# A new instruction order for a two-layer attention and FFN kernel, planned with a changed clock for GpSimd's port and for instruction fetches

## The chip, the core and the metric

The kernel runs on one core of a Trainium2 chip. A core has engines that work side by side, each from its own list of instructions: TensorE (PE, matrix products), VectorE (DVE), ScalarE (ACT), GpSimd (POOL), and SyncE (SP), which starts DMA transfers. An engine takes its instructions strictly in the order in which they stand. The metric is the device time of one execution in microseconds (us), the median over several.

## The reference

Two layers, each an attention over 2048 tokens in four segments of 512 tokens, with a memory that is carried from segment to segment, and a gated FFN. 32 heads have 16 values each; the model is 512 wide, the FFN 1792.

```python
for s in range(N):                               # 4 segments of 512 tokens
    qs, ks, vs = (q[:, :, s].copy(), k[:, :, s].copy(), v[:, :, s].copy())
    logits = jnp.einsum('bhqd,bhkd->bhqk', qs, ks) * scale + mask
    p = _softmax(logits, axis=-1)
    a_dot = jnp.einsum('bhqk,bhkd->bhqd', p, vs)
    pq = phi(qs)                                 # where(t > 0, t + 1, exp(t))
    num = jnp.einsum('bhld,bhde->bhle', pq, M)
    den = jnp.einsum('bhld,bhd->bhl', pq, z)[..., None] + 1e-06
    a_mem = num / den
    o = g * a_mem + (1.0 - g) * a_dot
    outs.append(o)
    pk = phi(ks)
    M = M + jnp.einsum('bhld,bhle->bhde', pk, vs)
    z = z + jnp.einsum('bhld->bhd', pk)
...
x = x + _A_ref(_layernorm(x, axis=-1), A_wq, A_wk, A_wv, A_wo, A_beta)
x = x + _B_ref(_layernorm(x, axis=-1), B_w_gate, B_w_up, B_w_down)   # gelu(x @ w_gate) * (x @ w_up) @ w_down
```

Both lines stand twice: the second layer uses the same weights.

## The kernel before

The work of a layer is cut into four segments of 512 tokens, so there are eight attentions (k = 0 to 7) and eight FFNs, numbered alike; k + 4 of the second layer needs the rows that FFN k has finished. All activations stay in the core's memory: `x_sb` holds the running sum, which every output product (`wo`, `down`) is added to.

What an attention k does: a layernorm (`xn`, turned into `xnT` by a DMA or by PE), products for q, k and v, 36 score rounds, taken in pairs, whose exponentials (`pt`) ScalarE makes, masks on `pt` by GpSimd (`affine_select`) or VectorE, and "flushes", products of `pt` with the values. VectorE turns a flush's result (`byq`, `ab`, `aT`). From the second segment of a layer on, the memory's part `amT` is added to `aT`, on VectorE or GpSimd (`on_dve_or_pool`, L1417): these are the sums of attention parts. The memory itself is updated by VectorE in four steps, `macc`, `zacc`, `mblk` and `zcols` (L1286 to L1305). Then come the output products `wo`; their result is added to `x_sb` either by a plain addition with separate statistics (L1463, L856, L859) or, for the first `quick` tiles, by an addition that also sums (L869, `mv` L873) and a square on ScalarE (`junk`, L876). FFN k follows: layernorm, 14 gate products, gelu on ScalarE, 14 up products, 4 output tiles of 14 products.

Nothing of the order is left to a scheduler. The function `order` runs the whole program once against a clock of its own, when the program is built, and emits each instruction when the clock says that its engine would take it. The class `Clocks` holds the time of PE; each other engine is an `Engine` with a list of jobs, from which `serve` takes the one with the least ready time plus slack. Where PE's clock finds no product ready, `order` emits a filling product of 128 columns on the tile `warm`. Three things of this clock matter here.

- A cost that is a `Port` stands for an operation on VectorE or GpSimd that needs the memory port which the planner takes them to share. `serve` lets it start only when the other engine's `port` time has passed (less 0.2 us). A `Port` marked `soft` (second argument) never holds up the other engine; it only makes it 0.15 us longer. A plain number needs no port.
- `Clocks.issue` counts PE's instructions in chunks of 256 (`CHUNK`). At `CHUNK_ASKED` in a chunk the next one is asked for, and at `CHUNK_END` PE waits until what was asked a chunk earlier has had `FETCH` us.
- The slacks and dues are not the same throughout: `POLICY` gives their first values, and `STAGES` a set of others for each window of 20 us (`WINDOW`) of PE's clock; `Policy.move` puts them in force. Among them are `turn_pe` (the FFNs whose `xn` PE turns), `quick`, `at_pool` (what GpSimd's slack is for an addition to `aT`) and `direct` (gates whose gelu reads PSUM).

An order once emitted is fixed. On the chip only semaphores decide when an instruction starts, so an operation that is longer there than in the planner's clock holds up everything behind it on its engine.

Of the kernel before, what the change touches and what calls it, by code (L numbers as in the profile page):

```python
# [37 lines left out]
CHUNK, CHUNK_ASKED, CHUNK_END, FETCH = 256, 178, 222, 3.7  # L38
# [27 lines left out]
def table(halved):  # L66
# [17 lines left out]
    if halved:  # L84
# [31 lines left out]
    rs_pool=32.757, f_urge=-233.244, quick=2, paired=8, turn_pe=1, turn_last=0, w_at=29.345, w_gap=2.17,  # L116
# [8 lines left out]
    park=3)  # L125
# [7 lines left out]
        rs_pool=2.667, quick=6, turn_pe=0, kb_slack=55.298, mem_slack=-32.756, e_q=-2.851, gelu_slack=-0.49,  # L133
        gate_step=78.038, up_due=-98.977, up_step=25.491, down_step=-53.827, upd_due=91.729, vz_slack=14.093,
        x_dve=7.459, direct=6, gelu_tiles=2, look=2.764, lag=0.475, xn_pool=30.206, cut_pool=102.189,
        at_pool=-237.424, gate_due=8.415, starve=1.292, soon=7.146, park=5)),
    (3, 4, dict(
        rs_pool=4.794, turn_pe=12, kb_slack=51.509, mem_slack=58.674, e_q=50.036, e_k=1.445, gelu_slack=1.935,
        gate_step=78.038, up_due=-96.513, up_step=85.14, down_step=-56.495, vz_slack=40.138, x_dve=6.187, direct=6,
        look=2.618, xn_pool=30.206, cut_pool=118.125, at_pool=-208.534, gate_due=14.291, shun=21.0, early=101.394,  # L140
        starve=0.321, soon=7.146, park=2)),
    (4, 5, dict(
        rs_pool=-2.341, quick=0, turn_pe=12, kb_slack=85.554, mem_slack=58.674, qk_due=1.009, e_q=50.137, e_k=1.464,
        gelu_slack=0.429, gate_step=79.294, up_due=-96.513, up_step=84.505, down_step=-72.139, vz_slack=51.333,
        x_dve=6.187, direct=3, gelu_tiles=2, xn_pool=20.238, cut_pool=148.746, at_pool=-208.534, gate_due=8.415,
        shun=21.0, early=101.394, starve=0.453, soon=7.146, park=2)),
    (5, 6, dict(
        rs_pool=36.794, quick=0, turn_pe=12, kb_slack=66.017, mem_slack=58.674, qk_due=1.009, e_q=55.15, e_k=2.984,
        gelu_slack=-0.805, gate_step=79.294, up_due=-96.513, down_step=-70.89, vz_slack=18.865, x_dve=7.455,
        gelu_tiles=2, look=2.835, lag=0.71, xn_pool=20.238, cut_pool=148.746, at_pool=-208.534, gate_due=0.276,  # L150
        shun=21.488, soon=7.146)),
    (6, 7, dict(
        rs_pool=11.417, f_urge=-261.392, quick=0, paired=11, turn_pe=0, flush_wait=0.581, piece_slack=36.524,
        kb_slack=76.591, mem_slack=-10.427, qk_due=-0.609, e_q=97.288, e_k=-5.757, exp_slack=-18.942, e_slack=69.536,
        phi_slack=30.587, gelu_slack=0.965, act_evict=1.166, gate_step=33.55, up_due=-80.509, down_due=-55.61,
        down_step=-81.567, upd_due=143.06, kb_act=60.08, vz_slack=4.039, x_dve=18.331, direct=0, gelu_tiles=2,
        look=2.622, lag=0.754, xn_pool=-3.088, kb_pool=116.679, cut_pool=153.155, at_pool=-189.709, gate_due=0.226,
        shun=85.539, hold=8, early=169.131, starve=0.31, near=101.522, cap=11, soon=0.694, kd_slack=37.99, park=6)),
    (7, 8, dict(
        rs_pool=-52.581, f_urge=-61.761, quick=3, paired=0, turn_pe=13, flush_wait=-3.039, piece_slack=92.516,  # L160
        kb_slack=220.906, mem_slack=57.517, qk_due=-30.647, e_q=-54.782, e_k=89.983, exp_slack=-17.861,
        e_slack=55.594, phi_slack=96.482, gelu_slack=214.751, act_evict=-149.173, gate_step=5.34, up_due=-0.69,
        up_step=3.923, down_due=12.354, down_step=-3.42, upd_due=-3.412, kb_act=75.691, vz_slack=-199.522,
        x_dve=3.843, direct=4, gelu_tiles=6, look=1.342, lag=0.004, xn_pool=-28.912, kb_pool=53.965, cut_pool=27.06,
        at_pool=-56.962, gate_due=-1.429, shun=104.852, hold=14, early=6.432, starve=57.777, near=-2.631, cap=0,
        soon=-55.855, kd_slack=-7.989, park=5)),
    (8, 9, dict(
        rs_pool=-52.581, f_urge=-145.617, quick=3, paired=0, turn_pe=9, flush_wait=-5.724, piece_slack=95.692,
        kb_slack=220.647, mem_slack=59.145, qk_due=-29.873, e_q=-54.782, e_k=89.76, exp_slack=-17.752,
        e_slack=55.641, phi_slack=95.445, gelu_slack=218.63, act_evict=-149.173, gate_step=5.34, up_due=-2.89,  # L170
        up_step=10.443, down_due=12.354, down_step=-3.42, upd_due=-3.412, kb_act=75.691, vz_slack=-188.382,
        x_dve=3.864, direct=5, gelu_tiles=6, lag=0.004, xn_pool=-26.431, kb_pool=53.965, cut_pool=27.06,
        at_pool=-56.962, gate_due=-1.429, shun=104.852, hold=14, early=6.432, starve=57.777, near=-2.631, cap=0,
        soon=-86.977, kd_slack=-7.989, park=5)),
    (9, 10, dict(
        rs_pool=-12.084, f_urge=-80.924, paired=7, turn_pe=0, flush_wait=-10.54, piece_slack=101.497,
# [20 lines left out]
        kd_slack=-0.609, park=5)),  # L197
# [1809 lines left out]
```

## Time and profile before

| | us |
|---|---|
| median of 3 executions | 538.3 (537.09 to 540.27) |
| the profiled execution | 536.81 |
| its span, first to last instruction | 535.1 |
| PE busy in it | 525.1 |
| ScalarE busy | 445.9 |
| VectorE busy | 433.7 |
| GpSimd busy | 268.1 |

The span is what the trace covers; the profiled execution's own time is 1.7 us longer. Matmuls are pipelined: one is shown busy until its modelled end while the next already runs, so busy PE is not PE at its peak, and a short pause can hide in it. In a row of the timeline the columns are start, duration, engine, line, operation, out<-in, and count, with the idle time before it and what ended that. In a row of groups they are line, engine, operation, shapes and count, then busy us and mean ns, then idle time before and its releasers. L541 is the line of a helper through which all products go, so PE's rows are told apart by their tiles. PE's granted clock was 1.00 throughout.

### The profile page before, as it was taken

The page shows a single profiled execution, that of the slowest core. Times are in us where ns is not written, and L with a number is a line of the kernel's source. Part 1 is how long each engine was busy: PE and PEld are TensorE (multiplying, and loading weights), DVE is VectorE, ACT ScalarE, POOL GpSimd, SP SyncE. Part 2 cuts the span into 40 slices and gives each one's busy share as a digit, 9 for nine tenths or more (in the row PEclk, how much of TensorE's full clock was granted, in tenths as well). Part 3 has the DMA queues.
Part 4 walks back from the last instruction along what each step waited for, and adds up shares of the span by engine and source line. Part 5 has one row for each costly group of instructions (what it writes and reads, how often), then busy time and mean ns, then how long its engine had stood idle before and what let it go on. Part 6 is the DMA issues. An engine that isn't in the chain of part 4 may idle for free.

```text
span 535.1 us, 24177 instructions
## 1 busy us (share of the span) xinstructions
PE 525.1 (98%) x10697; PEld 276.3 (52%) x10697; DVE 433.7 (81%) x823; ACT 445.9 (83%) x598; POOL 268.1 (50%) x333
## 2 busy tenths in 40 slices
PE   9999989998999999999999999999999999999997
PEld 4454455444545454555564544555555456555554
DVE  6899996999997999879987788888977997586342
ACT  6999989887999989899898899799989988952320
POOL 2986472568541966528773366491654354500000
PEclk9999999999999999999999999999999999999999
DMA  8366940323231232201221113310260132102101
GB/s 268 76 121 139 215 141 4 69 41 73 44 60 24 49 55 42 33 12 25 51 44 31 25 24 32 61 34 1 52 103 3 33 51 52 24 2 51 33 2 41
DMA packets 76762, 29.99 MB, mean 56 GB/s; under 512 B 61042, under 2 KB 76658, under 8 KB 76658
## 3 DMA queue, kind: packets, MB, share of 16 engines
q1 hardware_dynamic: 76368, 28.20, 26.0%
q8 instruction: 83, 1.36, 1.0%
q10 hardware_dynamic: 290, 0.26, 0.1%
q14 instruction: 21, 0.17, 0.1%
HBM read 9.70 MB, written 2.10 MB: 22 GB/s over the span
## 4 chain that ended last, share of the span: by engine, by line
PE 77%; DVE 4%; ACT 3%; POOL 1%; issue 1%; DMA 0%; ACTq 0%
PE ps L541 77%; ACT pt L1864 1%; ACT gel_sb L1616 1%; POOL kx L726 1%; DVE xn L920 1%; ACT gel_sb L1519 1%; POOL e L1170 1%; ACT gel_sb L779 0%; DMA xnT<-xn 0%; DVE x_sb L1463 0%; DVE st L856 0%; DVE mblk L1286 0%; DVE byq L1391 0%; DVE x_sb L869 0%; ACT L1519 0%
## 5 line engine op out<-in xcount | busy, mean ns | idle before, releaser
L1864 ACT ACTIVATE pt<-ps 128x1024 bf16<-128x1024 f32 x288 | 278.9, 1036 | 26.8 <-PE ps L541 19.9
L1813 POOL TENSOR_SCALAR_AFFINE_SELECT pt<-pt 128x256 bf16<-128x256 bf16 (+1 forms) x192 | 113.6, 604 | 148.0 <-ACT pt L1864 145.6
L541 PE MATMUL ps<-xnT,wg_sb 128*32 128x512 bf16 (+3 forms) x1367 | 107.7, 362 | 0.3 <-DMA xnT<-xn 0.3
L541 PE MATMUL ps<-wd_sb,gel_sb 128*32 128x512 bf16 (+2 forms) x1431 | 106.1, 354 | 0.0
L541 PE MATMUL ps<-xnT,wu_sb 128*32 128x512 bf16 (+1 forms) x1252 | 103.6, 379 | 0.2 <-ACT gel_sb L1519 0.2
L1557 DVE TENSOR_TENSOR gel_sb<-gel_sb,ps 128x512 bf16<-128x512 bf16 x112 | 75.2, 683 | 30.8 <-PE ps L541 28.5
L541 PEld LDWEIGHTS <-gel_sb 128*32 128x32 bf16 (+1 forms) x1623 | 53.2, 97 | 41.2 <-issue 2.2
L541 PEld LDWEIGHTS <-wu_sb 128*32 128x32 bf16 (+1 forms) x1252 | 45.8, 97 | 45.3 <-issue 2.0
L541 PEld LDWEIGHTS <-wg_sb 128*32 128x32 bf16 (+1 forms) x1367 | 47.5, 97 | 38.7 <-issue 1.5
L1391 DVE STREAM_TRANSPOSE byq<-ps 128x512 f32<-128x512 f32 x64 | 45.4, 710 | 24.5 <-PE ps L541 23.8
L1170 POOL TENSOR_SCALAR e<-e 128x512 bf16<-128x512 bf16 x32 | 50.0, 1565 | 7.1 <-ACT e L1147 6.4
L1463 DVE TENSOR_TENSOR x_sb<-x_sb,ps 128x512 bf16<-128x512 bf16 (+1 forms) x54 | 34.0, 635 | 17.8 <-PE ps L541 17.7
L1818 POOL TENSOR_SCALAR_AFFINE_SELECT pt<-pt 64x1024 bf16<-64x1024 bf16 x32 | 38.1, 1192 | 17.8 <-ACT pt L1864 15.6
L541 PE MATMUL ps<-xnT,wk_sb 128*32 128x512 bf16 (+2 forms) x330 | 34.9, 377 | 0.7 <-ACT pt L1864 0.7
L541 PE MATMUL ps<-pt,vaug 128*32 128x256 bf16 (+2 forms) x1344 | 35.1, 239 | 0.1
L541 PE MATMUL ps<-wv_sb,xnT 128*32 128x512 bf16 (+1 forms) x227 | 32.4, 380 | 2.2 <-DVE x_sb L1463 1.8
L541 PE MATMUL ps<-xnT,wq_sb 128*32 128x512 bf16 (+2 forms) x339 | 34.0, 377 | 0.0
L1616 ACT ACTIVATE gel_sb<-gel_sb 128x1024 bf16<-128x1024 bf16 (+4 forms) x31 | 33.3, 1157 | 0.0
L541 PE MATMUL ps<-q,kx 32*128 32x64 bf16 (+2 forms) x1120 | 31.4, 217 | 0.6 <-ACT pt L1864 0.3
L541 PEld LDWEIGHTS <-vaug 128*32 128x32 bf16 x1344 | 27.2, 97 | 9.2 <-issue 1.6
L856 DVE BATCH_NORM_STATS2 st<-x_sb 128x6 f32<-128x512 bf16 x46 | 31.2, 679 | 0.4
L541 PEld LDWEIGHTS <-kx 32*128 32x128 bf16 x1120 | 16.8, 92 | 28.1 <-issue 27.4
(128 smaller groups left out, 722.1 us busy)
## 6 DMA issues: line engine op xcount, KB each, us to landing
vz<-vaug SPq DMA_DIRECT2D x14, 136.0 KB, 3.0
wg_sb<-in_B_w_gate_dram SPq DMA_DIRECT2D x8, 224.0 KB, 4.0
wu_sb<-in_B_w_up_dram SPq DMA_DIRECT2D x8, 224.0 KB, 3.9
wd_sb<-in_B_w_down_dram SPq DMA_DIRECT2D x7, 256.0 KB, 5.7
x_sb<-in_A_x_dram SPq DMA_DIRECT2D x3, 512.0 KB, 6.5
out_dram<-x_sb SPq DMA_DIRECT2D x12, 128.0 KB, 1.9
xnT<-xn SPq DMA_TRANSPOSE x56, 2.5
kx<-kf SPq DMA_DIRECT2D x12, 64.0 KB, 3.3
```

The lines of the kernel that those rows point to most:

```text
L541: self.nc.tensor.matmul(*args, **kw)
L726: return lambda: eng.tensor_scalar(out=kx[:, :, C * which:C * which + n], in0=kf[:, :, 0:n], scalar1=masks[:, which:which + 1], scalar2=No ...
L856: nc.vector.bn_stats(out=self.st6[:, 0, :], in_=x_sb[:, self.tt0 + j, :])
L920: eng.tensor_scalar(out=xn[:], in0=x_sb[:, self.tt0 + j, :], scalar1=self.mv[:, j, 1:2] if self.wide else self.mv[:, j, 0:1], scalar2=self ...
L1170: lambda eng: eng.tensor_scalar(out=e[0][:], in0=e[0][:], scalar1=1.0, scalar2=None, op0=ALU.min), summed)
L1391: nc.vector.transpose(out=(self.byq[:, pars[0], :, :].rearrange("p a c -> p (a c)") if h is None else self.byq[:].rearrange("p u a c -> p ...
L1463: ck.dve.post(ck.made(), slack, (0.15 + 0.00104 * (c1 - c0), lambda: nc.vector.tensor_tensor(out=xt, in0=xt, in1=ps()[:, 0:c1 - c0], op=AL ...
L1557: ck.dve.post(ck.made(), NORMAL, (0.683, lambda: nc.vector.tensor_tensor(out=g, in0=g, in1=ps()[:], op=ALU.mult), lambda t: (ps.read(t), e ...
L1616: return (0.205 + 0.427 * (f1 - f0), lambda: nc.scalar.activation(out=g, in_=g, func=ACT.Gelu_apprx_tanh), lambda t: self.gelu_done(t, f0, ...
L1813: nc.gpsimd.affine_select(out=view, in_=view, pattern=[[0, 4], [0, n], [1, C]], compare_op=ALU.is_ge, fill=0.0, base=C, channel_multiplier=-1)
L1818: nc.gpsimd.affine_select(out=view, in_=view, pattern=[[0, 4 * TPS], [1, C]], compare_op=ALU.is_ge, fill=0.0, base=0, channel_multiplier=-1)
L1864: nc.scalar.activation(out=pt_all[:, s0:s0 + 2, 2 * p:2 * p + 2, :].rearrange("p r h c -> p h r c"), in_=ps_all[:, pair[0]:pair[1] + 1, :] ...
```

## The change

Four entries of the planner's clock are other (`CHUNK_END`, `FETCH` and two costs), and with them the table `STAGES` from its second row on, that is from 40 us of PE's clock. The operations of the program are the same; who does some of them, and the order of nearly all, is not.

```diff
-CHUNK, CHUNK_ASKED, CHUNK_END, FETCH = 256, 178, 222, 3.7
+CHUNK, CHUNK_ASKED, CHUNK_END, FETCH = 256, 178, 216, 4.2
...
     (4, 5, dict(
-        rs_pool=-2.341, quick=0, turn_pe=12, kb_slack=85.554, mem_slack=58.674, qk_due=1.009, e_q=50.137, e_k=1.464,
...
+        rs_pool=26.539, f_urge=-179.403, quick=0, paired=11, turn_pe=14, flush_wait=-38.498, piece_slack=30.144,
...
-                             (0.154, lambda: nc.vector.tensor_tensor(out=zacc[:], in0=zacc[:], in1=self.zk[:],
+                             (Port(0.154), lambda: nc.vector.tensor_tensor(out=zacc[:], in0=zacc[:], in1=self.zk[:],
                                                                      op=ALU.add), kept)]
...
-                    on_dve_or_pool(t, slack, pol.at_pool, Port(0.15 + 0.275 * part), Port(0.16 + 1.0 * part, True), add, there)
+                    on_dve_or_pool(t, slack, pol.at_pool, Port(0.15 + 0.275 * part), Port(0.16 + 1.0 * part), add, there)
```

GpSimd's addition to `aT` thus holds the port in the clock for its whole length, and the sum of `zacc` waits for the port. The new file has eight lines more in the table, so every later line number is eight higher (L1417 is now L1425).

Counted in the two lists: PE has 21,396 rows before and 20,776 now; matmuls on the whole array 1,048 and 1,194, on four column tiles 7,600 and 7,144, on four row tiles 2,049 in both; changes between these 294 and 303; transposes by PE 32 and 48; fillings after the start 13 and 17. GpSimd has 13 and 14 additions to `aT`, VectorE 11 and 10. VectorE copies `kf` from PSUM 17 and 10 times, ScalarE 11 and 18; ScalarE's squares are 14 and 18, its gelus over gathered tiles 31 and 38. SP has 56 and 52 transposing DMAs for `xnT`. Up to PE's matmul 1005 the lists are the same.

The first place is VectorE after attention 1's memory sum. Before, in VectorE's list (`r`, `ab`, `aT`: the flush's result; `xn`: rows of a layernorm):

```order
L1401 RECIPROCAL r<-byq 128x32
L1407 TENSOR_TENSOR ab<-byq,r 128x2x16x16
L1414 STREAM_TRANSPOSE aT<-ab 128x512
L1303 TENSOR_TENSOR macc<-macc,ps 128x128
L920 TENSOR_SCALAR xn<-x_sb,mv,rs 128x512
L1305 TENSOR_TENSOR zacc<-zacc,zk 128x4
L1286 TENSOR_TENSOR mblk<-macc,bd 128x512
L1463 TENSOR_TENSOR x_sb<-x_sb,ps 128x512 x3
```

GpSimd's list at the same place, where the addition waits for the transposed `aT`:

```order
L899 TENSOR_TENSOR rs<-ve,mhalf 128x2
L1813 AFFINE_SELECT pt<-pt 128x4x128
L1417 TENSOR_TENSOR aT<-aT,amT 128x512
L1818 AFFINE_SELECT pt<-pt 64x1024 x2
L1813 AFFINE_SELECT pt<-pt 128x4x64 x2
```

Now the memory's three steps stand ahead of that, in VectorE's list (`phiq`: the q of the memory's product):

```order
L1399 STREAM_TRANSPOSE byq<-ps 128x512
L1471 TENSOR_TENSOR x_sb<-x_sb,ps 128x512
L1311 TENSOR_TENSOR macc<-macc,ps 128x128
L1313 TENSOR_TENSOR zacc<-zacc,zk 128x4
L1294 TENSOR_TENSOR mblk<-macc,bd 128x512
L1159 SCALAR_TENSOR_TENSOR phiq<-q,e 128x512
L1300 TENSOR_TENSOR zcols<-bd,zacc 128x32
```

`macc`, `zacc` and `mblk` follow each other with nothing between, and the `xn` is gone from there. The last flush of attention 1 comes some twenty rows later, in VectorE's list, and two `xn` still stand behind its `aT`, to which GpSimd's addition is tied:

```order
L1409 RECIPROCAL r<-byq 128x32
L1415 TENSOR_TENSOR ab<-byq,r 128x2x16x16
L1422 STREAM_TRANSPOSE aT<-ab 128x512
L928 TENSOR_SCALAR xn<-x_sb,mv,rs 128x512 x2
L1159 SCALAR_TENSOR_TENSOR e,zk<-kf,e 128x512
L877 SCALAR_TENSOR_TENSOR x_sb,rowsum<-ps,x_sb 128x512
L881 TENSOR_TENSOR mv<-rowsum,means 128x2
```

The additions to `x_sb` behind it are now those that also sum.

The second place is PE at the output products of attention 1. Before (`wv_sb`: value products of attention 4; rows between are left out):

```order
L541 MATMUL ps<-wo_sb,aT 128x512
...
L541 MATMUL ps<-q,kx_122 128x192
...
L541 MATMUL ps<-wv_sb,xnT 128x512
...
L541 MATMUL ps<-pt,vz 32x64
...
L541 MATMUL ps<-xnT,wq_sb 32x512
```

Now (`warm`: fillings; `ident`: transposes by PE):

```order
L549 MATMUL ps<-wv_sb,xnT 128x512
...
L549 MATMUL ps<-warm 128x128
...
L549 MATMUL ps<-wo_sb,aT 128x512
...
L549 MATMUL ps<-q,kx_122 128x192
...
L549 MATMUL ps<-warm 32x128
...
L549 MATMUL ps<-xnT,wq_sb 32x512
...
L549 MATMUL ps<-zcols,phiq 32x8
...
L553 MATMUL ps<-ident,xn 128x128
```

Nine fillings stand among the output and value products (in four groups), and FFN 1's four tiles are turned by PE, with 16 transposes, where SP turned them by DMA.

More of the change, by code (lines that the diff above doesn't have):

```diff
@@ L152 @@
-    (6, 7, dict(
[L153 to L158, printed above, removed]
@@ L159 @@
-    (7, 8, dict(
[L160 to L166, printed above, removed]
@@ L167 @@
-    (8, 9, dict(
[L168 to L174, printed above, removed]
```

320 lines of the change are left out of this document (174 added, 146 removed).

## The prediction

> **What bounds the kernel now.** I read the page's busy times first, then the windows, then PE's own waits, then the stretches in which PE waited.
>
> ```profile
> span 535.1 us, 24177 instructions
> PE 525.1 (98%) x10697; PEld 276.3 (52%) x10697; DVE 433.7 (81%) x823; ACT 445.9 (83%) x598; POOL 268.1 (50%) x333
> ...
> 0.00:62.00 62.00, 59.78 (x1004) 30.02 (x1005) 53.06 (x122) 57.15 (x88) 41.00 (x63) 1.00 0.67 158
> 62.00:200.00 138.00, 133.73 (x2693) 68.72 (x2695) 124.87 (x241) 125.47 (x171) 79.03 (x92) 1.00 0.29 62
> 200.00:520.00 320.00, 319.76 (x6738) 170.30 (x6733) 252.35 (x457) 263.29 (x340) 148.06 (x179) 1.00 0.19 35
> 520.00:536.00 16.00, 11.87 (x276) 7.28 (x268) 3.46 (x6) 0.00 (x0) 0.00 (x0) 1.00 0.11 36
> ```
>
> PE is the bound. In the windows the third number is its busy time: 320 us from 200 to 520 hold 0.24 us of idle PE, and 62 to 200 hold 138.00 - 133.73 = 4.27. Up to PE's matmul 1005 (at about 62 us) the two orders are the same, so the 2.22 idle before it stay, and so does the tail after 520, where the last product, its addition and its store end the run. What an order can win is therefore 4.27 + 0.24 = 4.5 us of visible idle, and it must pay for any work that it adds to PE.
>
> ```profile
> PE ps L541 <- DVE x_sb L1463: 1.8, 1, 1.8
> PE ps L541 <- issue: 1.2, 2, 1.0
> PE ps L541 <- ACT pt L1864: 0.5, 2, 0.3
> PE ps L541 <- DMA xnT<-xn: 0.3, 1, 0.3
> ```
>
> These are PE's waits from 62 to 200 (total, times, longest). Two kinds make 3.0 of the 4.27: one wait for VectorE, and two in which PE waited for nothing that the profile shows, which I take for instructions not yet fetched.
>
> **The port.** The wait for VectorE, first VectorE (DVE), then GpSimd (POOL), then PE:
>
> ```profile
> 126.62 1.29 DVE L920 TENSOR_SCALAR xn<-x_sb,mv,rs 128x512 bf16<-128x512 bf16 x1
> 127.83 1.09 DVE L1305 TENSOR_TENSOR zacc<-zacc,zk 128x4 f32<-128x4 f32 x1
> 129.17 1.62 DVE L1286 TENSOR_TENSOR mblk<-macc,bd 128x512 bf16<-128x512 f32 x1
> 130.71 1.27 DVE L1463 TENSOR_TENSOR x_sb<-x_sb,ps 128x512 bf16<-128x512 bf16 x2
> ...
> 126.61 1.15 POOL L1417 TENSOR_TENSOR aT<-aT,amT 128x512 bf16<-128x512 bf16 x1 [0.31 <-DVE aT L1414]
> 127.72 2.53 POOL L1818 TENSOR_SCALAR_AFFINE_SELECT pt<-pt 64x1024 bf16<-64x1024 bf16 x2
> ...
> 127.61 0.40 PE L541 MATMUL ps<-q,kx 32*128 32x64 bf16 x12
> 127.94 1.68 PE L541 MATMUL ps<-wo_sb,aT 128*128 128x512 bf16 x7
> 131.44 1.46 PE L541 MATMUL ps<-wv_sb,xnT 128*128 128x512 bf16 x6 [1.82 <-DVE x_sb L1463]
> ```
> ```profile
> L920 DVE TENSOR_SCALAR xn<-x_sb,mv,rs x58: 330/408/1292, 6.0 to 488.0; 128x512 bf16<-128x512 bf16 x58
> L1305 DVE TENSOR_TENSOR zacc<-zacc,zk x4: 115/156/1087, 127.8 to 408.2; 128x4 f32<-128x4 f32 x4
> L1286 DVE TENSOR_TENSOR mblk<-macc,bd x6: 667/852/1620, 75.9 to 408.9; 128x512 bf16<-128x512 f32 x6
> L1417 POOL TENSOR_TENSOR aT<-aT,amT x13: 1152/1155/1165, 102.0 to 455.1; 128x512 bf16<-128x512 bf16 x13
> ```
>
> Under GpSimd's addition xn took 1.29 against its median 0.408 (+0.88); under the two masks zacc took 1.09 against 0.156 (+0.93) and mblk 1.62 against 0.852 (+0.77). That is 2.58 us on VectorE, whose next work, the additions that empty PSUM banks, then came late by 1.82 for PE. The old planner held the addition for harmless to VectorE and zacc for an operation without the port. The new one knows both, and its order puts macc, zacc and mblk elsewhere. The term is -1.82 at most and 0 at least, for the wait may only move; GpSimd even gets one such addition more, 14 for 13, and behind one of them two xn still follow. I take -1.8, since macc, zacc and mblk now stand one behind the other, ahead of the two flushes there. The Trainium skill (SBUF — State Buffer, section "SBUF: two separate sides") calls the port that the two engines share an exclusive lock for the whole instruction. By that rule xn would have lost all of the addition's remaining 1.14 us, where the row says 0.88; the rule's price per collision is thus the higher one, and the term, a wait of PE that is measured as such, would not change by it.
>
> **Fetches.**
>
> ```profile
> q8 instruction: 83, 1.36, 1.0%
> ...
> 74.92 0.29 PE L541 MATMUL ps<-q,kf 16*128 16x64 bf16 x7
> 76.20 0.36 PE L541 MATMUL ps<-q,kf 16*128 16x192 bf16 x5 [0.99 <-issue]
> ...
> 124.24 0.83 PE L541 MATMUL ps<-wo_sb,aT 128*32 128x512 bf16 x12 [0.21 <-issue]
> ```
>
> 83 packets feed PE's list of 21,396 rows, one for some 258 rows; the list is now 20,776 rows long. A score round was cut in two for 0.99 us, and 0.21 went before a product; both followed many short matmuls. With the rates below, the poorest stretches of 147 matmuls (the planner's distance from asking to needing) held 2.8, 2.9 and 3.3 us of work in the old order after 62 us and 3.4, 4.1 and 4.3 in the new. So the term is -1.2, with 0 as the other bound: a fetch also competes with data.
>
> **What PE gets to do.** Seven products of 512 columns took 1.68 us (row at 127.94), the last of them 0.380:
>
> ```profile
> L541 PE MATMUL ps<-wo_sb,aT 128*128 128x512 bf16 x65 | 15.2, 380 | 0.0
> L545 PE MATMUL ps<-ident,xn 128*128 128x128 bf16 x32 | 3.2, 231 | 0.0
> ```
>
> (1.68 - 0.38) / 6 = 0.217 for 512 columns. Twelve score matmuls, four abreast, are 512 columns; from 127.61 to the next start at 127.94 went 0.33, so a change of the array's tiling cost 0.33 - 0.217 = 0.11. The new order has 16 more transposes by PE (FFN 1's four tiles, which were DMA transposes) and 4 more filling matmuls, 20 x 128 columns = five products: +1.09. It changes tiling 303 times for 294: 9 x 0.11 = +1.0. Products that went from four column tiles to the whole array (456 small matmuls fewer, 114 products) stream the same columns: 0.
>
> **Where PE is let run dry.** Filling matmuls mark places where the planner had nothing for PE. Before, eleven stood in one place, here the last of three groups:
>
> ```profile
> 70.50 0.55 PE L541 MATMUL ps<-warm 128*128 128x128 bf16 x7
> ...
> 71.93 0.29 PE L541 MATMUL ps<-q,kx 32*128 32x64 bf16 x7 [0.26 <-ACT pt L1864]
> ```
>
> Now six are left there and nine stand around attention 4's first values and FFN 1's first products, where the 1.82 were lost. Beside them I put the 0.26 of this row: +0.3, bounds 0 and 1.82 (the old wait, foreseen but not avoided).
>
> **Covered.** VectorE hands seven copies of kf to ScalarE, where four more squares and a finer split of the gelus stand too. By 62 to 200 ScalarE is busy 125.47 of 138.00 and VectorE 124.87; this is hidden as long as the exponentials keep ahead, and the new order spreads them: 384 of the 512 groups of four score matmuls are out after 345 us of PE work, by the rates above, instead of 326. SP's transposes are four fewer. If that cover is gone, PE waits for score banks as it did for 0.5 us in the waits above; I cost it at 0, bounds -0.5 and +1.
>
> **The sum:** +1.09 + 1.0 + 0.3 - 1.8 - 1.2 = -0.6 us on a span of 535.1. The other pauses (4.5 - 3.0 = 1.5) I leave as they are, since each order makes new ones.
>
> **Rivals.**
>
> Faster: all idle after 62 us goes. -4.5 + 2.1 of work = -2.4, and a little more, because part of a pause hides in the modelled end of the product before it: after 127.94 seven products last 7 x 0.217 = 1.52, so PE lost 131.44 - 129.46 = 1.98 where the row says 1.82. Eight pauses of 0.16 make 1.3: -3.7 in all. For it speaks that from 200 to 520 the old planner lost 0.24; against it that in 62 to 200, where VectorE and ScalarE are 90% busy, it could not.
>
> Slower: the chain in front of FFN 1's first products becomes the bound.
>
> ```profile
> L869 DVE SCALAR_TENSOR_TENSOR x_sb<-ps,x_sb 128x512 bf16<-128x512 f32 x14 | 9.6, 683 | 1.2 <-PE ps L541 1.1
> L873 DVE TENSOR_TENSOR mv<-rowsum,means 128x2 f32<-128x2 f32 x14 | 3.0, 214 | 0.5
> L778 DVE CAST vaug<-ps 128x512 bf16<-128x512 f32 x12 | 8.2, 687 | 1.9 <-PE ps L541 1.6 <-ACT pt L1864 0.2
> L1151 DVE SCALAR_TENSOR_TENSOR phiq<-q,e 128x512 bf16<-128x512 bf16 x24 | 18.2, 763 | 0.6 <-POOL e L1170 0.4
> ```
>
> Behind the last output product VectorE's new queue holds one addition (0.683 + 0.214), a copy of values (0.687), a phiq (0.763), a copy of q (about 0.687) and four xn (4 x 0.408): 4.7 us. PE's list holds, from that product to its transposes, four value, eight q and four k products, a flush of 1280 columns and one round of scores: 19.5 x 0.217 and three changes of tiling, 4.6, and sixteen very short denominators. There is hardly any slack, so every xn or phiq that GpSimd's port holds up (about 0.9 each) reaches PE, and ScalarE's square may come late too. Four such collisions, here and at the other segments, give -0.6 + 3.5 = +2.9; from there it is slower. GpSimd's share of 50% speaks for some of them, the planner's better knowledge against four.
>
> No effect of the port's rule: the new waits are as long as the old one, so -1.8 falls away: +1.2, still no change that can be told.
>
> **How the numbers follow.** The profiled execution took 536.81 (its span and 1.7 around it), the three shown 537.09, 538.3 and 540.27; the middle of all four is 537.7, 0.6 under the median shown, and I add to that. The sum gives 537.1, the faster rival 534.0, the slower 540.6, the last 538.9. Chances: sum 0.33, port without effect 0.12, faster 0.25, slower 0.30. A measurement of this kernel tells about 0.5% (2.7 us) from no change, so no change 0.45, faster 0.25, slower 0.30. The likeliest case's own range is 535.6 to 539.5. The range for 8 in 10 is 533 to 542.5: below, all pauses gone and the added work 1 us cheaper; above, five or six collisions.
>
> **What would show it.** Right: PE's busy share stays at 98%, its list shows about 2 us more work, no issue wait near 1 us after 62, and no wait for VectorE over 1 us between the output products of attention 1 and FFN 1's gates; xn, zacc and mblk keep near their medians there. Wrong: idle PE from 62 to 200 over 6 us, or idle over 2 us after 200, where the old order had almost none and every stage is ordered anew; then the new order lost what the old one had by luck. Zero idle in 62 to 200 would make the faster rival right.

## The result and the profile after

The changed kernel takes 539.26 us (median of 22 executions, 537.50 to 542.31), the kernel before 537.03 (22 executions, 535.93 to 540.27). The ratio is 1.0039 with a 95% interval of 1.0026 to 1.0053: slower by 0.4%. The prediction said 537.1 us, slightly below a base of 537.7. Ratios here and below leave disturbed executions out, so they can differ from the quotient of two medians, by up to 0.15 points of a per cent in the table below.

The page of the changed kernel, and its windows (start and end, then length, then the busy time of PE, weight load, VectorE, ScalarE and GpSimd, PE's clock, share and rate of DMA):

```profile
span 536.9 us, 23550 instructions
PE 525.5 (98%) x10387; PEld 275.6 (51%) x10387; DVE 430.9 (80%) x823; ACT 450.8 (84%) x620; POOL 257.3 (48%) x330
...
q8 instruction: 81, 1.33, 1.1%
...
xnT<-xn SPq DMA_TRANSPOSE x52, 3.0
```
```profile
62.00:200.00 138.00, 135.81 (x2562) 68.27 (x2560) 121.12 (x242) 126.18 (x177) 79.90 (x90) 1.00 0.28 57
200.00:520.00 320.00, 317.16 (x6519) 169.47 (x6522) 251.38 (x454) 267.20 (x357) 136.74 (x177) 1.00 0.19 35
```

Idle PE from 62 to 200 us fell from 4.27 to 2.19, and from 200 to 520 it rose from 0.24 to 2.84: 5.03 where 4.51 stood. The span grew by 1.8 us; both kernels are at the same matmul at 62 us, so this arose behind it: some 1.3 of it is busy time of PE and 0.5 is idle time. The last row shown, from the page's list of transfers, says where the idle time comes from: a transposing DMA now lands 3.0 us after its issue (median), where the same row before said 2.5:

```profile
xnT<-xn SPq DMA_TRANSPOSE x56, 2.5
```

PE's waits in the changed kernel, first for 62 to 200, then for 200 to 520, name it:

```profile
PE ps L549 <- DMA xnT<-xn: 1.4, 1, 1.4
PE ps L553 <- DVE xn L928: 0.3, 1, 0.3
```
```profile
PE ps L549 <- DMA xnT<-xn: 2.1, 2, 1.1
PE ps L549 <- ACT gel_sb L1527: 0.4, 1, 0.4
PE ps L549 <- ACT pt L1872: 0.2, 1, 0.2
```

The wait of 1.8 for VectorE and the two that were put down to "issue" are gone; 3.5 us of waits for `xnT` stand where 0.3 stood. The three places, on the timeline:

```profile
123.51 1.05 PE L549 MATMUL ps<-wv_sb,xnT 128*32 128x512 bf16 x16 [1.39 <-DMA xnT<-xn]
...
206.50 0.81 PE L549 MATMUL ps<-xnT,wg_sb 128*128 128x512 bf16 x3 [1.02 <-DMA xnT<-xn]
...
266.38 1.81 PE L549 MATMUL ps<-xnT,wg_sb 128*128 128x256 bf16 x15 [1.11 <-DMA xnT<-xn]
```

They are the first values of attention 4 and the first gates of FFN 2 and FFN 3. VectorE's memory steps, on the other hand, run undisturbed:

```profile
109.61 0.25 DVE L1311 TENSOR_TENSOR macc<-macc,ps 128x128 f32<-128x128 f32 x1
109.78 0.16 DVE L1313 TENSOR_TENSOR zacc<-zacc,zk 128x4 f32<-128x4 f32 x1
109.90 0.69 DVE L1294 TENSOR_TENSOR mblk<-macc,bd 128x512 bf16<-128x512 f32 x1
```

`zacc` took 1.09 and `mblk` 1.62 at that place before. GpSimd is at work beside them too (`e`, 109.20 to 110.68), but with neither an addition to `aT` nor a mask.

**Why the transposes are late.** The DMA records of the trace give the start of each packet of 16,384 bytes on the instruction queue (q8 above, 81 packets), that is, of each fetch for PE. Four transposes in the new order have a consumer that is ready some 3.4 to 3.9 us after the issue; the order before has three that are closer still (2.1 to 2.5). All four met a fetch, none of the three did in this profile, one of them by 0.03 us: its fetch started at 2.53, just behind the landing at 2.50. "Fetch" is the time from the transpose's issue to the start of the fetch:

```
               issued at   fetch    landed after
after            118.55    2.56       4.92        attention 4's values wait
                 126.60    2.01       4.15
                 201.94    2.37       4.42        FFN 2's gates wait
                 261.75    2.53       4.58        FFN 3's gates wait
before           142.15    none       2.43
                 197.24    2.53       2.50
                 264.01    none       2.44
```

The same over 16 traces of these two orders (the two kernels and 14 of the runs below), transposes of `xnT` after 100 us:

```
fetch starts behind the issue    count   landed: median (10% to 90%)   over 3 us
not from -0.6 to 2.7 us            277   2.44 (2.41 to 2.51)                 5
-0.6 to 0.5                         61   3.08 (2.46 to 3.78)                35
0.5 to 1.5                          85   3.50 (3.15 to 4.20)                85
1.5 to 2.2                          76   4.14 (3.98 to 4.38)                76
2.2 to 2.7                          63   2.45 (2.41 to 4.58)                16
```

Of 161 transposes with a fetch 0.5 to 2.2 us behind their issue, all took more than 3 us; of 277 without one, 5 did. The critical ones of both orders lie at the edge, 2.2 to 2.7, where the same transpose lands early in one execution and late in the next: the one before FFN 2 took 4.42 in the profile above and 2.45 in a second profile of the same kernel. The clock of the planner does know of these collisions (`Clocks.landing`), but only while the fetch starts 0.74 to 2.44 us behind the issue, so nothing keeps it from putting transposes right behind that edge. The mechanism shows in the landings. A landing is sixteen steps of a semaphore, as many as there are DMA engines, and the fetch is one packet of 0.9 to 2.1 us. Of the transpose issued at 201.94 fifteen steps had come after 2.43 us and the last came after 4.42; of the one at 261.75, fifteen after 2.44 and the last after 4.58. Of the 92 landings over 3 us with a fetch 1.5 to 2.7 us behind the issue 66 are like that, with fifteen steps inside 3 us: one engine's share is late, the other fifteen are not. That it is the engine which carries the fetch is inferred, since the records don't name a packet's engine; and the last step comes some 1.1 us after the fetch has ended, which they don't explain. With a fetch 0.5 to 1.5 us behind the issue all sixteen steps are late (the first after more than 2.6 us in all 85, where 2.29 is usual without a fetch), so more than one held engine is at work there, and what it is stays open. That a fetch delays a transpose is shown; how it does is shown only in part.

### The profile page after: what moved, and what is told of

The parts are those of the page before. It is cut to its first block, busy times and chain, and to the rows that moved or that the text cites. A ratio compares the mean times of both kernels' runs of the same rounds, so it can differ in the third digit from the quotient of the medians.

```text
span 536.9 us, 23550 instructions
## 1 busy us (share of the span) xinstructions
PE 525.5 (98%) x10387; PEld 275.6 (51%) x10387; DVE 430.9 (80%) x823; ACT 450.8 (84%) x620; POOL 257.3 (48%) x330
## 4 chain that ended last, share of the span: by engine, by line
PE 80%; DVE 7%; ACT 5%; DMA 4%; issue 2%; POOL 1%; SPq 0%; ACTq 0%; DVEq 0%; POOLq 0%
PE ps L549 80%; DMA xnT<-xn 2%; ACT pt L1872 2%; DVE xn L928 1%; DVE byq L1399 1%; ACT gel_sb L1527 1%; ACT gel_sb L1624 1%; DMA wu_sb<-in_B_w_up_dram 1%; DVE x_sb L877 1%; DVE st L864 1%; DVE ab L1415 1%; DMA x_sb<-in_A_x_dram 1%; PE ps L553 0%; DVE x_sb L1471 0%; ACT L1527 0%
## 5 line engine op out<-in xcount | busy, mean ns | idle before, releaser
L1821 POOL TENSOR_SCALAR_AFFINE_SELECT pt<-pt 128x256 bf16<-128x256 bf16 (+1 forms) x192 | 111.9, 595 | 160.0 <-ACT pt L1872 146.4
L549 PE MATMUL ps<-xnT,wg_sb 128*32 128x512 bf16 (+3 forms) x1229 | 105.1, 354 | 2.3 <-DMA xnT<-xn 2.1
L549 PEld LDWEIGHTS <-wu_sb 128*32 128x32 bf16 (+1 forms) x1171 | 44.1, 97 | 45.3 <-issue 1.6
L1178 POOL TENSOR_SCALAR e<-e 128x512 bf16<-128x512 bf16 x31 | 48.2, 1558 | 1.9 <-ACT e L1155 1.0
L1471 DVE TENSOR_TENSOR x_sb<-x_sb,ps 128x512 bf16<-128x512 bf16 (+1 forms) x50 | 31.3, 634 | 19.7 <-PE ps L549 19.4
L1826 POOL TENSOR_SCALAR_AFFINE_SELECT pt<-pt 64x1024 bf16<-64x1024 bf16 x28 | 32.5, 1159 | 18.8 <-ACT pt L1872 17.9
L549 PE MATMUL ps<-wv_sb,xnT 128*128 128x512 bf16 (+1 forms) x188 | 31.4, 380 | 1.9 <-DMA xnT<-xn 1.4
L1624 ACT ACTIVATE gel_sb<-gel_sb 128x512 bf16<-128x512 bf16 (+3 forms) x38 | 32.6, 932 | 0.0
L549 PE MATMUL ps<-wo_sb,aT 128*32 128x512 bf16 (+1 forms) x248 | 30.8, 380 | 0.0
```

Of the source, the lines that this page charges most:

```text
L549: self.nc.tensor.matmul(*args, **kw)
L1178: lambda eng: eng.tensor_scalar(out=e[0][:], in0=e[0][:], scalar1=1.0, scalar2=None, op0=ALU.min), summed)
L1471: ck.dve.post(ck.made(), slack, (0.15 + 0.00104 * (c1 - c0), lambda: nc.vector.tensor_tensor(out=xt, in0=xt, in1=ps()[:, 0:c1 - c0], op=AL ...
L1624: return (0.205 + 0.427 * (f1 - f0), lambda: nc.scalar.activation(out=g, in_=g, func=ACT.Gelu_apprx_tanh), lambda t: self.gelu_done(t, f0, ...
L1821: nc.gpsimd.affine_select(out=view, in_=view, pattern=[[0, 4], [0, n], [1, C]], compare_op=ALU.is_ge, fill=0.0, base=C, channel_multiplier=-1)
L1826: nc.gpsimd.affine_select(out=view, in_=view, pattern=[[0, 4 * TPS], [1, C]], compare_op=ALU.is_ge, fill=0.0, base=0, channel_multiplier=-1)
```

## The experiments

Theory 1: the loss is the meeting of fetches and close transposes, a matter of the phase in which the fetches (one for 256 rows of PE's list) fall against the work. Theory 2: the loss lies in the order itself (late `xn`, VectorE, SyncE), and the fetch is beside the point. Theory 3: traffic of other DMAs. All medians and ratios, each beside the kernel before on the same chip:

| run | median, us | before, us | ratio (95%) |
|---|---|---|---|
| changed kernel again | 539.19 | 536.61 | 1.0044 (1.0030 to 1.0058) |
| after_m12 | 537.86 | 536.90 | 1.0003 (0.9984 to 1.0022) |
| after_p12 | 537.29 | 536.90 | 1.0008 (0.9994 to 1.0021) |
| after_m30 | 538.80 | 536.61 | 1.0038 (1.0025 to 1.0051) |
| after_p226 | 537.20 | 536.63 | 1.0016 (1.0006 to 1.0026) |
| after_p206 | 537.59 | 536.51 | 1.0017 (1.0002 to 1.0031) |
| after_p186 | 537.94 | 536.63 | 1.0036 (1.0015 to 1.0056) |
| before_m12 | 537.31 | 536.90 | 1.0003 (0.9990 to 1.0016) |
| before_p12 | 537.23 | 536.90 | 1.0009 (0.9994 to 1.0024) |
| before_m30 | 538.45 | 536.61 | 1.0023 (1.0006 to 1.0040) |
| before_p226 | 536.14 | 536.63 | 0.9999 (0.9990 to 1.0008) |
| before_p48 | 540.71 | 536.61 | 1.0065 (1.0044 to 1.0086) |
| before_add_dve | 535.62 | 536.63 | 0.9995 (0.9977 to 1.0014) |
| before_best | 536.28 | 536.51 | 1.0000 (0.9985 to 1.0015) |
| clock_only | 548.23 | 536.51 | 1.0207 (1.0189 to 1.0225) |
| table_only | 563.45 | 536.51 | 1.0496 (1.0472 to 1.0521) |

**Moving the fetches by twelve rows.** Nothing is changed but rows that no one reads. For later fetches the first six filling products are planned and not emitted (in both kernels):

```diff
+        if not self.silent:
             self.nc.tensor.matmul(*args, **kw)
...
+                te.silent = len(ck.fills) < 6
                 product(ps()[:, 0:P], warm[:], wide[:, 0, :])
+                te.silent = False
```

For earlier ones, products that the planner does not count stand ahead of the program (six in the p12 runs, 24 in before_p48):

```diff
     keep_warm(WARM, 0)
+    for _ in range(6):
+        nc.tensor.matmul(ps_all[:, 0, 0:32], lhsT=warm[:], rhs=wide[:, 0, 0:32], start=True, stop=True)
```

> The changed kernel without its first six filling products (they stand where TensorE waits anyway, at about 71 us, and nothing reads them), so every later row of TensorE's list stands 12 rows earlier in the list and each fetch of 256 rows comes about 12 rows, some 0.33 us, later against the work around it. Everything else is the same list. Theory 1 (a transposing DMA lands 2 us late when a fetch for TensorE starts up to some 2.6 us behind its issue): behind the three transposes whose consumers waited (issued at 118.55, 201.94, 261.75) the fetch then starts at 2.9, 2.7 and 2.85 us instead of 2.56, 2.37 and 2.53; at least two of the three land after about 2.5 instead of 4.4 to 4.9, the waits for xnT of 3.5 us in all fall below 1.5, and the time is 2 to 3.5 us below the changed kernel's. Theory 2 (xn, made by VectorE, or SyncE's queue is late, and the fetch is beside the point): the three waits stay at about 3.5 us and the time does not move. Theory 3 (traffic of other DMAs on the same queues): as theory 2.

> The changed kernel with six products of 32 columns more ahead of the program (they read the warm-up tile, nothing reads their result), so that every fetch comes 12 rows, some 0.33 us, earlier against the work. Theory 1: the fetches start at about 2.2, 2.0 and 2.2 us behind the three transposes, which is still inside the stretch in which they collide: the waits for xnT stay between 2.5 and 4 us, time within 1 us of the changed kernel's. Theories 2 and 3: the same, no move.

> The kernel before with the same six products ahead of the program. Theory 1: two transposes that landed 2.50 and 2.41 us behind their issue at 197.24 and 205.36, with the fetch starting at 2.53 in both, now have it at about 2.2, so they land at 3.5 to 5 us and their consumers wait: TensorE's waits for xnT rise from 0.3 us to 1.5 to 3, and the time by 1.5 to 3.5 us. Theories 2 and 3: waits for xnT stay below 0.5 us and the time moves by less than 0.5.

> The kernel before without its first six filling products: fetches 0.33 us later. Theory 1: the two transposes at 197.24 and 205.36 have the fetch at 2.85 and stay at 2.5 us; no new wait over 0.5 us for xnT, time within 1 us of the kernel before. Theories 2 and 3: no move either.

Both shifts took the changed kernel from 1.0044 to 1.0003 and 1.0008, some 2 us (by the medians beside the kernel before, 1.3 to 1.6 us for the first and 1.8 to 2.2 for the second). By the ratio the first is the least that theory 1 called for, by the medians it falls short of it; the second is against theory 1's expectation, which was no move. Theories 2 and 3 are out for this part of the loss, since the order of all work and of all other transfers was the same and both had expected no move. Tile by tile it fitted only in part. With fetches twelve rows later the three fetches came 2.45, 2.35 and 2.50 us behind their transposes, not 2.9, 2.7 and 2.85, so a fetch doesn't follow its row at a fixed distance; FFN 2's transpose landed after 2.44, the other two after 4.58 and 4.55, and 2.9 us of waits were left in that execution. In the kernel before, the earlier fetch did what was expected in the execution that was profiled, the slowest of its twelve (539.93):

```profile
201.38 2.24 PE L541 MATMUL ps<-xnT,wg_sb 128*32 128x256 bf16 x36 [2.37 <-DMA xnT<-xn]
```

The transpose that had landed after 2.50 took 4.25 with the fetch at 1.99, and FFN 2's gates, which had waited 0.30, waited 2.37. The median rose by 0.3 us only, which I read as most executions staying on the good side of the edge. This execution paid twice. Behind the wait the granted clock of PE was halved: the windows of this trace show 0.50 from 202.0 to 204.5 us, and the clock's own record has half speed for 3.41 us, which is worth some 1.7 us by an estimate from that record. Its 2.7 us above the median are therefore not the wait alone.

The fetch wait of the kernel before (0.99 in the middle of a round of twelve score products at 76.20, after seven of them) moved with the rows. With fetches twelve rows later, it stands six products further on, behind the other five and one gate product:

```profile
74.69 0.40 PE L544 MATMUL ps<-q,kf 16*128 16x64 bf16 x12
75.02 0.39 PE L544 MATMUL ps<-xnT,wg_sb 128*32 128x512 bf16 x1
76.17 1.04 PE L544 MATMUL ps<-xnT,wg_sb 128*32 128x512 bf16 x15 [0.77 <-issue]
```

In the run with 48 rows more below, it stands 24 products earlier, after fifteen gate products (76.06). So the "issue" of the prediction was a fetch, as it had been taken to be.

**Larger shifts.** First 30 rows later (nine warm-up products left out beside the six fillings) and, for the kernel before, 48 rows earlier.

> The changed kernel itself once more, so that it stands beside the next three on the same chip. All theories: 539.3 us, within 0.7, and at least two of the four transposes whose consumer stands right behind them (issued near 118.5, 126.6, 201.9, 261.8 us) land after more than 4 us.

> The changed kernel without nine of its twelve warm-up products before the first work and without its first six filling products at 71 us (nothing reads either): every fetch comes 30 rows later against the work, some 0.8 us in column products; the order is otherwise the same. Theory 1, worked out tile by tile from the changed kernel's trace: the four transposes with a consumer right behind them then have the fetch at 2.8 to 3.4 us and land after about 2.45, so the 4.1 us that TensorE lost before their consumers nearly all go: waits for xnT below 0.8 us in all, time 535.8 (535 to 536.8), below the kernel before. Theory 2 (the change's loss lies in the order itself: late xn, VectorE, SyncE): waits for xnT of 2 us and more stay, time above 538.

> The kernel before with 24 products of 32 columns more ahead of the program: fetches come 48 rows earlier. Theory 1, from the trace of the kernel before: its three transposes with a consumer right behind (142.15, 197.24, 264.01) and the last one at 492.1 now all meet a fetch and cost 1.8 + 2.1 + 1.4 + 0.9 us, of which 0.5 to 1.3 us is already paid in some executions: 541 us (539.5 to 542.5). Theory 2: 537 to 537.7 us, for the work in front of the first product is hidden by the wait for x.

> The kernel before with the same thirty rows left out as in the changed kernel's run beside it: fetches 30 rows later. Theory 1: its close transposes stay clear of fetches, one at 197.24 for good: 536.5 us (535.7 to 537.2). Theory 2: 536.9 us. This run is the fair partner of the changed kernel without its thirty rows: with the fetches out of the way on both sides, the predicted sum (TensorE's work +2.1, the two fetch waits and the wait for VectorE -3.0) should show as the changed kernel 0 to 1.5 us below.

The 48 rows cost the kernel before 4.1 us, as forecast, but by another road: in the profiled execution one of the four close transposes paid (at 264.27, landed after 4.63 with the fetch at 2.59, a wait of 1.3), and two fetches came late for PE itself:

```profile
60.04 1.04 PE L541 MATMUL ps<-xnT,wq_sb 128*32 128x512 bf16 x15 [1.32 <-issue]
76.06 1.25 PE L541 MATMUL ps<-xnT,wg_sb 128*32 128x512 bf16 x17 [0.81 <-issue]
```

The 30 rows helped neither kernel, and made the one before slower by 0.23%. Theory 1's times, 535.8 and 536.5, were missed by 3.0 and 2.0 us, though in the changed kernel two of the three waits for `xnT` were gone (1.8 us left, for attention 4's values). Both paid at the start: with three warm-up products, the first transposes run slowly (first the changed kernel, then the same without its rows):

```profile
6.41 0.40 PE L553 MATMUL ps<-ident,xn 128*128 128x128 bf16 x4 [1.07 <-DVE xn L928]
...
1.10 1.46 PE L552 MATMUL ps<-warm 128*128 128x512 bf16 x3 [1.10 <-DVE warm L647]
6.43 0.61 PE L556 MATMUL ps<-ident,xn 128*128 128x128 bf16 x4 [3.87 <-DVE xn L934]
6.83 0.42 PE L552 MATMUL ps<-warm 128*128 128x256 bf16 x1
```

Four transposes took 0.61, where the changed kernel has 0.40, the next three groups of four took 0.63 instead of 0.39, and the first key products started at 8.75 instead of 7.80 us. So the same phase was made the other way round, by adding 226 rows of a cycle of 256 (and 186, for 70 rows later):

```diff
+    te.silent = True
     keep_warm(WARM, 0)
+    te.silent = False
+    for _ in range(125):
+        nc.tensor.matmul(ps_all[:, 0, 0:48], lhsT=warm[:], rhs=wide[:, 0, 0:48], start=True, stop=True)
```

> The run without nine warm-up products showed TensorE cold at its first transposes (four in 0.63 us, not 0.40), so that it paid something before any transpose that is in question. Here the same shift of 30 rows is had the other way round: the twelve warm-up products of 512 columns become 125 of 48, 226 rows more, which of a cycle of 256 is 30 rows later. Theory 1: the start costs nothing (first transposes near 6.4 us at 0.40 for four), the waits before FFN 2 and FFN 3 and at 126.6 (1.09, 1.17 and 0.3 us) go, the one for attention 4's values stays (its transpose stands behind four copies of keys and met a fetch in every phase so far): 536.7 us (535.9 to 537.6). Theory 2: 539.2.

> Twelve warm-up products of 512 columns become 105 of 56: fetches 70 rows later. Theory 1: as before, and the fetch at 122.8 us falls behind the landing of attention 4's first transpose too, so that its wait shrinks from 1.4 to 1.8 to below 0.7; a wait of 0.3 for the last transpose at 495 may come: 535.7 us (534.8 to 537). Theory 2: 539.2.

> The kernel before with 125 warm-up products of 48 columns for twelve of 512: fetches 30 rows later. Theory 1: its close transposes stay clear, 536.5 us (535.7 to 537.2); where the cold start was the reason that the same shift cost 1.8 us, that is gone. If it is again 538 or more, the shift itself costs the kernel before something and theory 1's table of tiles is wrong for it.

At 30 rows later the changed kernel was 2 us faster (537.2, within the range that theory 1 gave), the waits before FFN 2 and FFN 3 were gone, and the one for attention 4's values stayed:

```profile
124.03 1.05 PE L552 MATMUL ps<-wv_sb,xnT 128*32 128x512 bf16 x16 [1.46 <-DMA xnT<-xn]
```

The kernel before took 536.14, so the 1.8 us that it had lost without its 30 rows was the cold start; in the traces of these two runs its first flush product starts at 28.14 without the rows and at 26.50 here, and FFN 0's first gate product at 74.32 and 72.69. At 70 rows later attention 4's first transpose had the fetch at 3.36, landed after 3.10 and cost nothing: no wait for `xnT` is left in that profile. The time was not 535.7, though, but 537.94, with executions up to 541.43: at 51 us, in a stretch where the two orders agree, PE now stood still for 1.24.

```profile
51.26 1.05 PE L552 MATMUL ps<-wv_sb,xnT 128*32 128x512 bf16 x16 [1.24 <-ACT pt L1879]
```

The row names ScalarE. I read it as a fetch: its packet started at 47.78, among loads of weights, took 2.09 us and so ended at 49.87, and PE went on 1.39 later, as it went on 1.30 after the packet's end in the kernel before (74.90 to 76.20). The weight loads of the same products wait 1.36 us for "issue", which fits. The executions over 541 us are not explained by this wait alone: their granted clock was 0.997, where the profiled execution has 0.999.

A phase between the two, 50 rows later with 115 warm-up products of 52 columns:

> The changed kernel with 115 warm-up products of 52 columns for twelve of 512: fetches 50 rows later, between the two phases tried (30 rows later 537.2 us with 1.5 us of waits for attention 4's first transpose; 70 rows later none of those, but a fetch that took 2.09 us at 47.8 and a wait of 1.24 behind it). Theory 1: attention 4's first transpose has the fetch at 3.0 to 3.2 us and lands at about 3.1, its second with the fetch near 1.8 at 4.1: the wait is below 0.7; if the fetch before 62 us is not late, 536.2 us (535.4 to 537.2). Theory 2: 537.2 or more, the same waits.

This fetch came at 2.70, not at 3.0 to 3.2; the transpose landed after 4.92, the wait was 1.89 and the time 537.59, the expectation's other branch. For theory 3 the DMA records add a part: in the new order four copies of keys stand directly ahead of this transpose in SP's queue, and its packets start some 2.5 us behind its issue, when those copies' packets are through, so the stretch in which a fetch can catch them lies later. Without a fetch in it the transpose still landed after 3.10, which nobody waited for. The copies alone were not taken away, so their share is read, not shown: theory 3 stays open for this one wait.

**The port.** GpSimd's third addition to `aT` in the kernel before is given to VectorE, in its place:

```diff
+                    added.append(eng is nc.gpsimd)
+                    if eng is nc.gpsimd and sum(added) == 3:
+                        eng = nc.vector
```

> The kernel before, with GpSimd's third addition to aT (at 126.61 us) given to VectorE, everything else in its place. Theory P (the addition's hold of the port made VectorE late): xn takes 0.4 instead of 1.29, the addition costs VectorE some 0.45, the masks on GpSimd start 1.15 earlier and meet zacc and mblk less; TensorE's wait of 1.82 us for the additions to x_sb falls to 0.3 to 1.0 and the time by 0.8 to 1.5 us. Rival (the masks beside zacc and mblk are to blame): xn is short, but the wait stays above 1.4 and the time within 0.4 us.

```profile
127.04 0.41 DVE L920 TENSOR_SCALAR xn<-x_sb,mv,rs 128x512 bf16<-128x512 bf16 x1
127.36 0.15 DVE L1306 TENSOR_TENSOR zacc<-zacc,zk 128x4 f32<-128x4 f32 x1
127.44 1.30 DVE L920 TENSOR_SCALAR xn<-x_sb,mv,rs 128x512 bf16<-128x512 bf16 x1
127.45 2.88 POOL L1822 TENSOR_SCALAR_AFFINE_SELECT pt<-pt 64x1024 bf16<-64x1024 bf16 x2 [1.20 <-ACT pt L1868]
128.66 0.67 DVE L1287 TENSOR_TENSOR mblk<-macc,bd 128x512 bf16<-128x512 f32 x1
129.98 1.46 PE L541 MATMUL ps<-wv_sb,xnT 128*128 128x512 bf16 x6 [0.42 <-DVE x_sb L1467]
```

The wait fell from 1.82 to 0.42 and the median by 1.0 us (the ratio alone does not tell it from no change). But a mask met the second `xn`, which took 1.30. With the fetches 30 rows later besides:

> The kernel before with both repairs that the runs point to and its own order: GpSimd's third addition to aT on VectorE, and the fetches 30 rows later (125 warm-up products of 48 columns). If the two gains add (1.0 for the addition; 0.5 for the phase): 535.0 us (534.3 to 535.8), below both kernels. If they do not, 535.6 to 536.2.

```profile
126.05 2.56 POOL L1829 TENSOR_SCALAR_AFFINE_SELECT pt<-pt 64x1024 bf16<-64x1024 bf16 x2 [0.98 <-ACT pt L1875]
126.19 1.09 DVE L1313 TENSOR_TENSOR zacc<-zacc,zk 128x4 f32<-128x4 f32 x1
127.20 0.40 DVE L927 TENSOR_SCALAR xn<-x_sb,mv,rs 128x512 bf16<-128x512 bf16 x1
127.53 1.62 DVE L1294 TENSOR_TENSOR mblk<-macc,bd 128x512 bf16<-128x512 f32 x1
...
129.80 1.45 PE L544 MATMUL ps<-wv_sb,xnT 128*128 128x512 bf16 x6 [1.62 <-DVE x_sb L1474]
```

The two repairs do not add: the masks now met `zacc` and `mblk`, and the wait was back at 1.62. So the rival of the port test is half right: the masks held VectorE up there as the addition had, and which operation pays depends on fractions of a microsecond.

**Clock and table apart.** The four entries with the old table, and the new table with the old entries; each gives an order of its own.

> The kernel before with the four new entries of the clock and its old table, so a third order. Its list has 25 rows of filling products instead of 11 and 21,522 rows instead of 21,396. Theory 1 (what counts is the work that the order gives to TensorE and which transposes and fetches happen to meet): TensorE's wait of 1.82 us for VectorE and the fetch wait of 0.99 go, the fourteen more places where it runs dry and new waits for xnT come: 539 us (537 to 542), no better than the change with its table. Rival (the clock's entries are the gain and the table spoils it): below 535.5.

> The changed kernel's table with the old four entries of the clock, a fourth order: 36 rows of filling products, 20,590 rows. Theory 1: it was not made for this clock, TensorE runs dry at more places and VectorE meets GpSimd's additions again: 541 us (538 to 545). Rival (the clock's entries cost the time, the table is good by itself): below 537.5.

The direction was as expected, the size far off: +2.1% and +5.0%, where 539 and 541 us would have been +0.5% and +0.8%. With the entries alone PE's waits are:

```profile
PE ps L541 <- ACT pt L1864: 4.1, 11, 0.7
PE ps L541 <- DVE warm L636: 1.1, 1, 1.1
PE ps L541 <- DVE byq L1391: 1.0, 1, 1.0
PE ps L541 <- DVE gel_sb L1557: 0.8, 2, 0.4
```

Eleven waits for exponentials, 4.1 us, where the kernel before had five of 1.5 in the whole run; its span is 546.5 us, and its granted clock was 0.53 from 138 to 145 us. Each part alone is slower than both kernels, and each gives yet another order, so the runs put neither gain or loss of the change down to one part. Where the 27 us of the other run went stays open.

## Why the prediction was wrong, step by step

**PE's work** (+2.4 with the fillings): busy PE after 62 us rose by some 1.3 us, the same sign and about half the size, in a window whose busy times are modelled; no run took it by itself.

**The port** (-1.8): right. No wait for VectorE is left between attention 1's output products and FFN 1's gates, and the three memory steps have their medians. The one addition that two `xn` follow did cost one of them 0.8 us (1.25 for 0.41, at 125.10), and no one waited for it. That VectorE's delay beside GpSimd made PE's wait is shown by the run with the addition on VectorE, 1.82 to 0.42; that it was the addition and not the masks behind it is not, for the wait came back at 1.62 when the masks met the same operations.

**Fetches** (-1.2): right as a term, and too narrow as an idea. The waits that PE itself had for instructions went. Whether the new entries or the phase removed them is not told apart: at another phase (70 rows later) one of 1.24 came back, as I read it. That the same packets delay other transfers was not in the sum; "a fetch also competes with data" stands there as a reason for a bound and was given no price.

**The step that failed** is "The other pauses (4.5 - 3.0 = 1.5) I leave as they are, since each order makes new ones". They became 5.0: 3.5 us of waits for `xnT` instead of 0.3. The prediction took SP's queue to be better off, with four transposes fewer, and never looked at how close the remaining ones stood to their consumers. The figures that told it were there in the trace of the kernel before, with three consumers 2.1 to 2.5 us behind their transpose:

```profile
DMA to landing us min/median/max: 2.4/2.5/4.2
```

The list of instructions showed that all these places were ordered anew.

What that step is worth can be split by the runs. At the phases that both kernels were run in besides their own (12 rows later, 12 earlier, 30 later in either way) the ratios of the changed kernel lie 0.00, -0.01, 0.15 and 0.17 points of a per cent above those of the kernel before, 0.4 us in the mean, and in none of the four did the sum's -0.6 show. (The expectation of 0 to 1.5 us below its partner, for the pair without thirty rows, came out 0.35 above.) So of the 2.2 us about 0.4 belongs to the order, where the sum said -0.6; with intervals of 0.5 to 1 us either way on each ratio, 0.4 can't be told from nothing; the wait for attention 4's first transpose, 1.2 to 1.9 us in all but one of the profiles of this order, is more than the difference. The other 1.8 us or so is the phase that the new list happens to have, which is luck: of the six phases that the changed kernel ran in its own was the slowest, and the kernel before, 48 rows from its own, took 540.71. That second part is shown by the shifts, the first is worked out from small differences.

**The rivals.** "Slower" had the right sign and the wrong mechanism: 540.6 by GpSimd's port in front of FFN 1. No wait for VectorE over 0.3 us came. The sign in the last paragraph, "idle over 2 us after 200, where the old order had almost none", is what came about: 2.84.

**The base.** 22 executions of the kernel before have their median at 537.03, not at 537.7 or 538.3; the three shown were high by chance, and the base was 0.7 us too high.

## What to carry to other kernels

Where one engine's list is long, count its instruction fetches as transfers: find the consumers that stand right behind a DMA, and see whether a fetch falls between issue and landing. Two orders should be compared at more than one phase of the fetches (some idle rows ahead of the program are enough), for here that phase moved one and the same order by up to 4 us, more than the change itself. A planner that steers past such collisions needs a margin on its edge, or it will place its work exactly where the executions scatter.

## What the hardware showed

A transposing DMA of 128 x 512 took 2.44 us from issue to landing (median of 277), and 3.5 to 4.1 if one packet of 16,384 bytes for PE's instructions started 0.5 to 2.2 us behind its issue. With the fetch later than 1.5 us mostly one of its sixteen landing steps was late, with an earlier one all of them. No row of the waits names the fetch: they name the transpose.

With three warm-up products instead of twelve all four groups of four transposes at the start lasted 0.61 to 0.63 instead of 0.39 to 0.40, while the column of PE's clock reads 1.00 in both. Twelve don't always do: in the profile of the kernel before the first group of four took 0.61 behind twelve warm-up products that lasted 5.30 us, where the changed kernel's lasted 4.23. The Trainium skill (TensorE: Matmul & The Clock Gate, section "Part 1: The HAM clock gate") says that the array runs at half its clock until it has been busy for some 3.4 us; these rows agree in kind, and the column does not show it.

A long wait can be followed by a second loss. Behind the wait of 2.37 us shown above the granted clock fell to half for 3.41 us; behind waits of 1.84 and 1.89 (30 rows left out, and 50 rows later) it stayed at 1.00. This is one trace, but of 67 executions of the kernel before that were timed beside these runs, the seven over 539 us are the seven with a mean clock of 0.996 or 0.997.

On VectorE the operations shown beside GpSimd's addition or its mask of 64 x 1024 lost 0.8 to 0.9 us, whichever they were: `zacc` 1.09 for 0.15, `xn` 1.30 for 0.41, `mblk` 1.62 for 0.85. This is no fixed price: in the changed kernel an `mv` under such a mask took 0.54 for 0.16 (130.73), and the memory steps beside GpSimd's `e` lost nothing (109.61).
